# u added at a chunk's opening group from blocks on chip, w2's pieces at 2 KB, low parts a product later

## The chip, the cores and the metric

The kernel runs on one core of a Trainium2 chip. A core has a matrix engine (TensorE, PE in the rows; its weight loads are PEld), three element-wise engines (VectorE = DVE, ScalarE = ACT, GpSimd = POOL), a queue that issues DMAs (SyncE = SP) and 16 DMA engines that carry them between HBM and the on-chip memory. SBUF holds tiles of 128 partitions, PSUM the sums that TensorE makes. Each engine works through its own instructions in order and waits on semaphores for the others. The metric is the device time of one execution in microseconds (us).

## What is computed

Inputs are float64 arrays read as pairs of 32-bit words. An attention with random features gives `x` (8 x 576 rows of 512), and a mixing network follows:

```python
def phi(x):
    h = np.einsum('bhsd,md->bhsm', x, omega) - np.sum(x * x, axis=-1, keepdims=True) / 2.0
    return np.exp(h - np.max(h, axis=-1, keepdims=True)) / np.sqrt(m)
# attn = phi(q) (phi(k)^T v) / (phi(q) sum(phi(k)) + 1e-6), heads side by side: x
h = x.transpose(0, 2, 1) @ U @ V          # U: 576 x 32, V: 32 x 576
u = x + h.transpose(0, 2, 1)
out = u + np.maximum(u @ w_ch1, 0.0) @ w_ch2   # w_ch1: 512 x 2048, w_ch2: 2048 x 512
```

## The kernel before

The first 440 us are the attention; it leaves the rows of `u` in HBM (`u_dram`). The rest is the two-layer network over six chunks of 768 rows. A float32 factor stands as a high part (ACT casts it to fp32r) and a low part (the rest), and each product is three passes of TensorE: high x high, high x low, low x high. A pass of 384 columns is one MATMUL row of the trace.

Chunks 0 and 1 keep w2 on chip; chunk 1 writes the weights of both layers, already split and combined, to HBM: `wx_dram` (first layer) and `w2x_dram` (second, by `seconds`). Chunks 2 to 5, some 590 us, are the stage that the change is mostly about. There both layers are done by a scheme of seven block products in place of eight, and all weights are streamed: each chunk loads 56 tiles `wx` and 56 tiles `wy` of 256 KB, 8 buffers of each.

A chunk is 8 passes p over w1's columns. In pass p `products2` makes seven products i = 0 to 6 into two PSUM banks (`p_s`, called X and Y). I number them n = 7p + i within the chunk. Between them come sums that DVE takes out of PSUM (`near`: u2, u3, c22, c21, c12, in the order of products 1, 3, 4, 5, 6), and from these, after a relu, eight operands T of the second layer, each split into a high part (`halves`: ACT) and a low part (`low`: DVE for T1 and T3, POOL for the other five of seven). The bank of product 4 is needed by product 6, so product 6 waits for DVE's sum c22; product 5 waits for u3; the next pass's product 0 waits for c21 and its product 1 for c12.

Two passes make a group g = p // 2. Its second layer (`Group.block`) is woven into the two passes after it: behind product n of those two passes stands block s = n mod 14, six matmuls of the i-th second-layer product for half j of the columns; the order of i is 1, 3, 2, 5, 7, 6, 4, each for j = 0 and 1. A block's PSUM bank is taken out by `evict` into accumulators `acc[i, j]` (a1 to a7 below; they lie in `w1f` and `acc`): ACT copies in group 0, DVE adds in groups 1 and 2. Two of the i's are held in PSUM over all groups (4 and 6; rows `p_r`). Group 3's blocks stand in passes 0 and 1 of the next chunk; there the a's are combined by DVE and POOL to the four output blocks, and `Output` fetches u's rows again from HBM (16 DMAs of 96 KB in 128-byte pieces a chunk), transposes the sums (`yt`, L1349 and L1353), adds them to u (`uraw`) and stores the result (16 DMAs in 128-byte pieces).

SP's queue is in program order. At the end of slot n it has one `wy` load (for the group two passes ahead: load number k of a group is issued at least six slots before the block that reads it), one `wx` load (for product n + 7), and what `follow(n)` puts there: in chunks 3 to 5 fetches of u at n = 0, 1, 12 and 13, stores at n = 12, 13, 17 and 19. A store that waits for DVE holds every load behind it.

## Time and profile before

| | |
|---|---|
| median of 2 runs | 1161.53 us (1160.68 to 1162.38) |
| the profiled execution | 1159.5 us, its span 1157.7 us |
| PE busy | 1066.5 us (92%) |
| DVE, ACT, POOL busy | 803.0 (69%), 595.5 (51%), 611.3 (53%) us |
| DMA queue q1 | 490880 packets, 231.22 MB, 78.0% of 16 engines' span |
| mean granted TensorE clock | 0.978 |

PE is nearly full on the mean, so a stage is read by what its matmuls wait for. "Busy" of a matmul includes the end of its pipeline: matmuls of 384 columns start every 0.17 us in a row without waits while each is shown 0.33 us long. In chunk 2 to 5 the passes start at these times: chunk 2 at 570.6, chunk 3 at 694.4, chunk 4 at 838.2, chunk 5 at 982.4 us; the last group's blocks stand alone from 1118.3 us on (the tail). A releaser in the rows is what ended a wait.

### The profile page before, as it was taken

To read this page: it belongs to the slowest core of one execution; us is meant where nothing else is said; L and a number is where in the kernel's file an instruction comes from. 1 tells how busy PE (TensorE), PEld (TensorE's weight loads), DVE (VectorE), ACT (ScalarE), POOL (GpSimd) and SP (SyncE) were. 2 spreads that over 40 slices of the span, in tenths; PEclk is the share of its full clock that TensorE was granted. 3 is DMA by queue.
4 is the path that set the end of the run, shared out by engine and by line. 5 is a ranking of instruction groups with operands and counts; after the bars stand their busy time and mean duration, and the time that the engine had idled before them with its cause. 6 is when DMAs were issued, how large, how long until landed. Compare 5 with 4: busy or idle time off the path is not lost. (4 is left out here: it accounts for less than half of the span.)

```text
span 1157.7 us, 19949 instructions
## 1 busy us (share of the span) xinstructions
PE 1066.5 (92%) x6447; PEld 999.1 (86%) x6447; DVE 803.0 (69%) x1543; ACT 595.5 (51%) x1521; POOL 611.3 (53%) x582
## 2 busy tenths in 40 slices
PE   8999999999999999999879999799996899969993
PEld 7999999999889897898769988688886798869983
DVE  4898989989877757776743687535876358763554
ACT  5999898998656534333435343333433334333330
POOL 3447466583455564777435547444474444744552
PEclk9999999999999999999999999999999999999996
DMA  8899897893145654986688999699996999959876
GB/s 137 146 177 146 188 163 150 188 142 99 70 142 158 145 116 149 284 294 232 215 298 236 238 310 247 140 238 248 310 252 144 235 241 319 252 133 278 283 170 129
DMA packets 493350, 232.78 MB, mean 201 GB/s; under 512 B 379840, under 2 KB 439232, under 8 KB 493248
## 3 DMA queue, kind: packets, MB, share of 16 engines
q1 hardware_dynamic: 490880, 231.22, 78.0%
q8 instruction: 52, 0.85, 0.3%
q10 hardware_dynamic: 2368, 0.30, 0.2%
q14 instruction: 50, 0.41, 0.1%
HBM read 183.21 MB, written 48.23 MB: 200 GB/s over the span
## 5 line engine op out<-in xcount | busy, mean ns | idle before, releaser
L1094 PE MATMUL p_s<-ux,wx 128*128 128x384 f32 x1344 | 281.3, 345 | 35.1 <-DVE near L810 26.7
L1094 PEld LDWEIGHTS p_s<-ux,wx 128*128 128x128 f32 x1344 | 239.0, 192 | 52.6 <-DVE near L810 36.0
L1235 POOL TENSOR_TENSOR t<-near,t 128x384 fp32r<-128x384 f32 x128 | 137.5, 1094 | 238.1 <-ACT t L1054 238.1
L1279 PE MATMUL p_o<-t,wy 128*128 128x384 f32 x960 | 199.6, 343 | 24.4 <-DMA wy<-w2x_dram 21.6
L1279 PEld LDWEIGHTS p_o<-t,wy 128*128 128x128 f32 x960 | 173.2, 193 | 29.0 <-DMA wy<-w2x_dram 19.2
L589 ACT ACTIVATE e<-p_p,nm 128x128 f32<-128x128 f32 x576 | 167.6, 390 | 22.4 <-DVE nm L582 14.1
L810 DVE TENSOR_TENSOR near<-p_s,near 128x384 f32<-128x384 f32 x200 | 110.0, 551 | 80.7 <-PE p_s L1094 73.5
L436 POOL TENSOR_TENSOR xl<-xT,xh 128x384 fp32r<-128x384 f32 x95 | 94.2, 1012 | 111.7 <-ACT xh L432 94.3
L1058 ACT ACTIVATE near<-near 128x384 f32<-128x384 f32 x64 | 33.6, 525 | 212.1 <-DVE near L810 212.1
L582 DVE TENSOR_REDUCE nm<-p_p 128x4 f32<-128x512 f32 x144 | 97.7, 679 | 21.0 <-PE p_p L576 11.7
L574 PE MATMUL p_p<-omh,xh 128*128 128x256 f32 x288 | 92.4, 321 | 1.2 <-ACT e L589 0.9
L1054 ACT CAST t<-near 128x384 fp32r<-128x384 f32 x160 | 82.1, 515 | 21.4 <-POOL near L810 13.2
L1279 PE MATMUL p_r<-t,wy 128*128 128x384 f32 x384 | 79.5, 341 | 6.1 <-DMA wy<-w2x_dram 6.1
L575 PE MATMUL p_p<-oml,xh 128*128 128x256 f32 x288 | 81.3, 282 | 0.0
L576 PE MATMUL p_p<-omh,xl 128*128 128x256 f32 x288 | 81.0, 282 | 0.0
L810 DVE TENSOR_TENSOR w1f<-p_o,w1f 128x384 f32<-128x384 f32 x96 | 53.0, 552 | 37.1 <-PE p_o L1279 37.0
L1279 PEld LDWEIGHTS p_r<-t,wy 128*128 128x128 f32 x384 | 68.8, 192 | 7.9 <-DMA wy<-w2x_dram 7.9
L1028 PE MATMUL p_s<-ux,wx 128*128 128x384 f32 x336 | 70.2, 344 | 4.8 <-DVE near L810 3.0
L1028 PEld LDWEIGHTS p_s<-ux,wx 128*128 128x128 f32 x336 | 61.2, 190 | 11.9 <-DVE near L810 4.6
L976 PE MATMUL p_p<-ux,wx 128*128 128x384 f32 x384 | 71.2, 336 | 0.2 <-DVE g L985 0.2
L532 PE MATMUL p_n<-kv,eT 128*128 128x65 f32 x512 | 71.3, 269 | 0.1
L183 POOL TENSOR_TENSOR mag<-mag,low 128x512 int32<-128x512 int32 (+2 forms) x35 | 45.1, 1288 | 47.5 <-DVE mag L161 42.3
(166 smaller groups left out, 2309.2 us busy)
## 6 DMA issues: line engine op xcount, KB each, us to landing
wx<-wx_dram SPq DMA_DIRECT2D x224, 256.0 KB, 4.7
wy<-w2x_dram SPq DMA_DIRECT2D x224, 256.0 KB, 4.6
raw<-in_moe_w_ch_dram SPq DMA_DIRECT2D x32, 512.0 KB, 4.4
wx_dram<-wx SPq DMA_DIRECT2D x56, 256.0 KB, 2.1
uraw<-u_dram SPq DMA_DIRECT2D x136, 96.0 KB, 4.5
u_dram<-x SPq DMA_DIRECT2D x36, 256.0 KB, 2.2
qt<-in_q_dram SPq DMA_DIRECT2D x120, 72.0 KB, 3.2
kt<-in_k_dram SPq DMA_DIRECT2D x52, 144.0 KB, 4.9
```

The lines of the kernel that those rows point to most:

```text
L436: rest.tensor_tensor(out=self.xl[-1], in0=self.turned, in1=f32(self.xh[-1]), op=ALU.subtract)
L574: nc.tensor.matmul(o, part.xh[g][:, ts], oh, start=True, stop=False)
L575: nc.tensor.matmul(o, part.xh[g][:, ts], ol, start=False, stop=False)
L576: nc.tensor.matmul(o, part.xl[g][:, ts], oh, start=False, stop=True)
L582: nc.vector.tensor_reduce(out=self.nm[:, :n], in_=self.pp[:, :n], axis=AX.X, op=ALU.max, negate=True)
L589: nc.scalar.activation(out=self.e[:, j, :], in_=self.pp[:, j, :], func=AF.Exp, bias=self.nm[:, j : j + 1])
L810: keep(engine.tensor_tensor(out=out, in0=a, in1=b, op=op))
L1028: keep(nc.tensor.matmul(o, l, r, start=(i in (0, 1, 4, 5) and k + j == 0), stop=(k == 1 and j == 2), skip_group_check=True,))
L1054: keep(nc.scalar.copy(out=T[i][:, 0], in_=x))
L1094: keep(nc.tensor.matmul(o, l, r, start=(i in (0, 1, 4, 5) and k + j == 0), stop=(k == 1 and j == 2), skip_group_check=True,))
L1235: keep(nc.gpsimd.tensor_tensor(out=l, in0=x, in1=h, op=SUBTRACT))
L1279: keep(nc.tensor.matmul(bank, l, r, start=(n + m == 0 and not (held and self.g)), stop=(n == 1 and m == 2 and (not held or self.g == LAST) ...
```

## The change

1. **u from blocks on chip.** A chunk's own transposed blocks of u lie in `w1f` until its pass 4. Group 0's evictions now add them: for i = 3, 2, 4, 5 DVE adds (or subtracts) the bank and a block, where ACT copied; for i = 7 ACT copies. Held in PSUM are now 1 and 6 instead of 4 and 6; 1's banks are copied by ACT at group 3 (`f1`), and POOL's sums of group 3 are rewritten (12 a chunk instead of 10). `Output` becomes `output`: transposes straight into the tile that is stored, no fetch, no add, at n = 11, 12, 15 and 17. In chunk 1 all six tiles of u are fetched before the stores, where two waited for stores of others.
2. **w2's pieces.** `w2x_dram` is laid out so that a `wy` load reads 2 KB a partition in one piece instead of twice 1 KB; chunk 1's writes go in 1 KB pieces instead of 2 KB.
3. **Low parts one product later.** DVE's low parts (of T1 and T3, and in passes 0 and 1 of chunks 3 to 5 T2's, which POOL had) are issued behind the next product's eviction, or at product 6 behind c12.
4. DVE's sums in SBUF take the form scalar_tensor_tensor (`exact`), and in chunk 1 four of seven operand splits go to POOL.

```diff
@@ split, sums
     def split(hl, x, rest=nc.gpsimd):
         keep(nc.scalar.copy(out=hl[:, 0], in_=x))
-        keep(rest.tensor_tensor(out=hl[:, 1], in0=x, in1=f32(hl[:, 0]), op=SUBTRACT))
+        if rest is nc.vector:
+            exact(hl[:, 1], x, f32(hl[:, 0]), SUBTRACT)
+        else:
+            keep(rest.tensor_tensor(out=hl[:, 1], in0=x, in1=f32(hl[:, 0]), op=SUBTRACT))
...
-    w2x_dram = [dram.tile([P, 2, 7, 2 * P], F32, name=f"w2x_dram{p}") for p in range(NH)]
+    w2x_dram = [dram.tile([P, 7, 2, 2 * P], F32, name=f"w2x_dram{p}") for p in range(NH)]
...
-            sums(self.s[i], a, b, op)
+            exact(self.s[i], a, b, op)
...
-            sums(self.total(i if self.c == 1 or i < 4 else 2), a, b, SUBTRACT, nc.gpsimd if self.c == 1 and i < 4 else nc.vector)
+            to = self.total(i if self.c == 1 or i < 4 else 2)
+            if self.c == 1 and i < 4:
+                sums(to, a, b, SUBTRACT, nc.gpsimd)
+            else:
+                exact(to, a, b, SUBTRACT)
...
-            split(slots[i], x, nc.vector)
+            split(slots[i], x, nc.gpsimd if self.c == 1 and i in (1, 3, 4, 6) else nc.vector)
@@ products2
-                low(rest, T[i][:, 1], x, f32(T[i][:, 0]))
+                step = lambda: low(rest, T[i][:, 1], x, f32(T[i][:, 0]))
+                if rest < 3:
+                    lows.append(step)
+                else:
+                    step()
...
-                    halves(2, c21, 3)
+                    halves(2, c21, third)
                 elif i == 6:
                     sums(c12, X, u2, ADD)
+                    while lows:
+                        lows.pop(0)()
...
-                evict = slot(i)
+                evict, due = slot(i), lows[:]
                 after(i)
                 if i in (0, 1) and pend:
                     pend.pop(0)()
                 evict()
+                for step in due if i < 6 else ():
+                    lows.pop(0)()
@@ Group
-                    keep(nc.sync.dma_start(out=f32(w), in_=w2x_dram[2 * self.g + n][:, :, PLACE[i], :]))
+                    keep(nc.sync.dma_start(out=f32(w), in_=w2x_dram[2 * self.g + n][:, PLACE[i]]))
...
-            held = i in (4, 6)
+            held = i in (1, 6)
...
         def evict(self, i, j, bank):
+            chunk = self.chunk
             if self.g < LAST:
+                if i in (1, 6):
+                    return
+                if self.g:
+                    sums(acc[i, j], bank, acc[i, j], ADD)
+                elif i == 7:
+                    keep(nc.scalar.copy(out=acc[i, j], in_=bank))
+                else:
+                    x = chunk.total(3) if i == 3 else chunk.block(*{2: (0, 0), 4: (1, 0), 5: (1, 1)}[i])
+                    sums(acc[i, j], bank, parted(x[:, j]), SUBTRACT if i == 3 else ADD)
                 return
+            a = {n: acc[n, j] for n in (2, 3, 4, 5, 7)}
+            pool = lambda x, y: sums(x, x, y, ADD, nc.gpsimd)
             if i == 1:
+                chunk.f1[j] = parted(dec.tile([P, HT], F32, name="f1", tag="mag", bufs=2))
+                keep(nc.scalar.copy(out=chunk.f1[j], in_=bank))
+                pool(a[2], chunk.f1[j])
+                pool(a[5], chunk.f1[j])
+            elif i == 6:
+                for n in (3, 5, 4):
+                    sums(a[n], bank, a[n], ADD)
             else:
+                sums(a[i], bank, a[i], ADD)
+                if i == 5:
+                    pool(a[3], a[5])
+                elif i == 7:
+                    pool(a[5], a[7])
+                    pool(a[7], chunk.f1[j])
+                    pool(a[4], a[7])
@@ follow, and the end
             def follow(n):
-                if n in (0, 1):
-                    out.fetch(n)
-                if n in (8, 9, 12, 13, 16, 17, 18, 19):
-                    out.add(*before.outs.pop(0), nc.vector)
-                if n in (12, 13):
-                    out.fetch(n - 10)
+                if n in (11, 12, 15, 17):
+                    output(c - 1, (11, 12, 15, 17).index(n))
...
+            group.T.append(now.products2(pairs, slot, between, low, pend, 2 if c > 2 and p < 2 else 3))
...
-    for m in range(4):
-        out.fetch(m, m > 1)
     for s in range(14):
         done.block(s)()
         next(loads, None)
+        if s in (11, 12):
+            output(NCH - 1, s - 11)
+    for m in (2, 3):
+        output(NCH - 1, m, True)
```

Three places of the order matter below. The first is SP's queue in passes 1 and 2 of chunk 3 (the others are alike): `out_dram` are stores of the chunk before, `uraw<-u_dram` the fetches of u, the `wx` and `wy` loads those for pass 2 on. Before:

```order
L1261 DMA wy<-w2x_dram_5403 128x2x256
L866 DMA wx<-wx_dram_5_5429 128x512
L1340 DMA out_dram<-uraw 32x24x32 x4
L376 DMA uraw<-u_dram_68 32x24x32 x4
L1261 DMA wy<-w2x_dram_5402 128x2x256
L866 DMA wx<-wx_dram_6_5430 128x512
L1340 DMA out_dram<-uraw 32x24x32 x4
L376 DMA uraw<-u_dram_68 32x24x32 x4
L1261 DMA wy<-w2x_dram_5403 128x2x256
L866 DMA wx<-wx_dram_0_5431 128x512
```

and in the change:

```order
L1355 DMA out_dram<-uraw 32x24x32 x4
L1279 DMA wy<-w2x_dram_5403 128x512
L869 DMA wx<-wx_dram_5_5429 128x512
L1355 DMA out_dram<-uraw 32x24x32 x4
L1279 DMA wy<-w2x_dram_5402 128x512
L869 DMA wx<-wx_dram_6_5430 128x512
L1279 DMA wy<-w2x_dram_5403 128x512
L869 DMA wx<-wx_dram_0_5431 128x512
```

The fetches between the loads are gone, and the first store stands one slot earlier, ahead of the loads of slot 12.

The second is DVE in pass 1 of chunk 3, from u3 (the first `near`) over c22 (the second) to c21 (the third). Before:

```order
L810 TENSOR_TENSOR near<-p_s,near 128x384
L810 TENSOR_TENSOR w1f<-p_r,w1f 128x384 x2
L810 TENSOR_TENSOR w1f<-p_r,w1f 128x2x192
L810 TENSOR_TENSOR near<-p_s,near 128x384
L1233 SCALAR_TENSOR_TENSOR t_9716<-near,t_9716 128x384
L810 TENSOR_TENSOR w1f<-p_r,w1f 128x384 x2
L810 TENSOR_TENSOR w1f<-p_r,w1f 128x2x192
L810 TENSOR_TENSOR near<-p_s,near 128x384
```

and in the change:

```order
L816 TENSOR_TENSOR near<-p_s,near 128x384
L816 TENSOR_TENSOR w1f<-p_r,w1f 128x384 x2
L816 TENSOR_TENSOR w1f<-p_r,w1f 128x2x192
L1251 SCALAR_TENSOR_TENSOR t_9656<-b_9593,t_9656 128x384
L816 TENSOR_TENSOR near<-p_s,near 128x384
L816 TENSOR_TENSOR w1f<-p_r,w1f 128x384 x2
L816 TENSOR_TENSOR w1f<-p_r,w1f 128x2x192
L1347 STREAM_TRANSPOSE uraw<-acc 128x384
L1347 STREAM_TRANSPOSE uraw<-w1f 128x384
L816 TENSOR_TENSOR near<-p_s,near 128x384
```

T1's low part (`t<-b`), which stood ahead of u3 two sums earlier, now stands between the sums of i = 6 (`p_r`, the third is a7 before and a4 now) and c22; T3's (`t<-near`) has gone behind c21, and two transposes of the output stand ahead of c21.

The third is POOL in the same pass, from the last low part of pass 0's operands on (`t`); `w1f` are its sums of group 3. Before:

```order
L1235 TENSOR_TENSOR t_11021<-near,t_11021 128x384
L810 TENSOR_TENSOR w1f<-w1f 128x384 x2
L1235 TENSOR_TENSOR t_11051<-near,t_11051 128x384
L810 TENSOR_TENSOR w1f<-w1f 128x384 x2
L1235 TENSOR_TENSOR t_11075<-near,t_11075 128x384
L810 TENSOR_TENSOR w1f<-w1f 128x384
L810 TENSOR_TENSOR w1f<-w1f 128x2x192
L810 TENSOR_TENSOR w1f<-w1f 128x384
L810 TENSOR_TENSOR w1f<-w1f 128x2x192
```

and in the change:

```order
L1253 TENSOR_TENSOR t_10985<-near,t_10985 128x384
L816 TENSOR_TENSOR w1f<-w1f 128x384
L1253 TENSOR_TENSOR t_11014<-near,t_11014 128x384
L816 TENSOR_TENSOR w1f<-w1f 128x384
L1253 TENSOR_TENSOR t_11037<-near,t_11037 128x384
L816 TENSOR_TENSOR w1f<-w1f 128x384
L816 TENSOR_TENSOR w1f<-w1f,f_10844 128x2x192
L816 TENSOR_TENSOR w1f<-w1f 128x2x192
L816 TENSOR_TENSOR w1f<-w1f 128x384
L816 TENSOR_TENSOR w1f<-w1f,f_10868 128x2x192
L816 TENSOR_TENSOR w1f<-w1f 128x2x192
```

DVE's third addition of half 0 (to a7 before, to a4 now) waits for POOL: counted from the `t` that opens the first of fourteen POOL operations in a row (t2, five slots earlier), its sum was the twelfth and is now the eleventh.

## Rows read from the trace of the kernel before

**Rows 1.** Table by stretch; columns in its first row; share is of DMA.

```profile
core 0: us, PE busy (x) PEld busy (x) DVE busy (x) ACT busy (x) POOL busy (x), PEclk, DMA share, GB/s
440.00:570.60 130.60, 125.00 (x607) 110.39 (x605) 98.50 (x158) 49.40 (x112) 86.38 (x81) 0.99 0.71 242
...
838.20:874.50 36.30, 30.82 (x168) 28.89 (x168) 26.07 (x42) 12.28 (x24) 26.06 (x24) 1.00 0.86 225
874.50:982.40 107.90, 94.68 (x504) 89.48 (x504) 62.59 (x107) 40.34 (x82) 47.67 (x42) 0.97 0.90 241
...
1018.80:1118.30 99.50, 91.20 (x504) 89.47 (x505) 51.97 (x92) 37.81 (x78) 45.75 (x43) 0.97 0.80 230
1074.70:1089.20 14.50, 14.50 (x85) 14.50 (x84) 8.05 (x14) 5.50 (x11) 7.63 (x8) 1.00 0.92 287
```

**Rows 2.** Waits of PE from 874.5 to 982.4: us in total, times, longest.

```profile
PE p_o L1279 <- DMA wy<-w2x_dram: 6.5, 3, 4.4
PE p_s L1094 <- DMA wx<-wx_dram: 2.8, 3, 2.1
```

**Rows 3.** SP's queue, chunk 4: start, us, line, transfer (xcount).

```profile
876.04 2.13 SPq L1340 DMA_DIRECT2D out_dram<-uraw  x4
880.83 2.02 SPq L376 DMA_DIRECT2D uraw<-u_dram  x4
...
891.67 0.54 SPq L1261 DMA_DIRECT2D wy<-w2x_dram  x1
```

**Rows 4.** PE in order of time, chunk 4; in brackets the idle time before.

```profile
870.91 1.32 PE L1094 MATMUL p_s<-ux,wx 128*128 128x384 f32 x6 [2.10 <-DVE near L810]
...
874.53 1.31 PE L1094 MATMUL p_s<-ux,wx 128*128 128x384 f32 x6 [1.24 <-DVE near L810]
...
894.99 1.33 PE L1279 MATMUL p_o<-t,wy 128*128 128x384 f32 x3 [4.42 <-DMA wy<-w2x_dram]
896.12 2.07 PE L1094 MATMUL p_s<-ux,wx 128*128 128x384 f32 x6
```

**Rows 5.** DVE in order of time, chunk 4, passes 0 and 1.

```profile
861.02 1.37 DVE L810 TENSOR_TENSOR uraw<-yt,uraw 128x384 f32<-128x384 f32 x1
862.31 1.36 DVE L1233 SCALAR_TENSOR_TENSOR t<-b,t 128x384 fp32r<-128x384 f32 x1
...
869.84 0.56 DVE L810 TENSOR_TENSOR w1f<-p_r,w1f 128x384 f32<-128x384 f32 x1 [0.52 <-POOL w1f L810]
870.31 0.55 DVE L810 TENSOR_TENSOR near<-p_s,near 128x384 f32<-128x384 f32 x1
...
872.53 1.48 DVE L810 TENSOR_TENSOR w1f<-p_r,w1f 128x384 f32<-128x384 f32 x3
...
874.85 0.57 DVE L1349 STREAM_TRANSPOSE yt<-w1f 128x384 f32<-128x384 f32 x1
```

**Rows 6.** POOL in order of time, the end of the chain of fourteen.

```profile
867.73 4.12 POOL L810 TENSOR_TENSOR w1f<-w1f 128x384 f32<-128x384 f32 x4
```

**Rows 7.** DMA queue 1131 to 1136, `wy` loads alone: packets, MB, share.

```profile
q1 hardware_dynamic: 1531, 1.36, 97.5%
```

**Rows 8.** DMA queue 589.5 to 592, nearly all 2 KB pieces.

```profile
q1 hardware_dynamic: 512, 0.93, 101.7%
```

**Rows 9.** DMA queue 1146 to 1156, stores in 128-byte pieces.

```profile
q1 hardware_dynamic: 11121, 1.40, 92.0%
```

**Rows 10.** DVE in chunk 2, pass 0.

```profile
588.99 0.69 DVE L1142 TENSOR_TENSOR u<-p_kv,u 128x512 f32<-128x512 f32 x1 [3.35 <-DMA u<-u_dram]
```

**Rows 11.** PE in chunk 1.

```profile
449.78 1.40 PE L1028 MATMUL p_s<-ux,wx 128*128 128x384 f32 x6 [1.77 <-DVE g L985]
```

**Rows 12.** Waits of PE in the tail, from 1118 on.

```profile
PE p_o L1279 <- DMA wy<-w2x_dram: 5.3, 1, 5.3
```

**Rows 13.** POOL in the tail.

```profile
1135.32 8.26 POOL L810 TENSOR_TENSOR w1f<-w1f 128x384 f32<-128x384 f32 x8 [8.25 <-DVE w1f L810]
```

**Rows 14.** SP in the tail.

```profile
1144.03 4.95 SPq L1340 DMA_DIRECT2D out_dram<-uraw  x8
```

## What the change should do to the time, and why

> **What bounds the kernel now.** I read the table by stretch first, to see where PE loses time, then what ended its waits there, and then the queues of the engines that it waited for. All comparisons go by a stretch's own clean pass: in chunk 5 a pass of 84 matmuls runs without a wait in 14.50 us [rows 1]. A chunk of eight would take 116 us; chunks 3, 4 and 5 take 143.8, 144.2 and 135.9 us by the pass starts above. So PE's waits in these three cost some 76 us, and that is the target, not PE's mean of 92%.
>
> In chunk 4 the two halves lose differently [rows 1]. Passes 0 and 1 take 36.3 us for 29.0 clean, over by 7.3, at a clock of 1.00. Passes 2 to 7 take 107.9 for 87.0, over by 20.9, and chunk 5's take 99.5, over by 12.5. Chunk 3 differs from chunk 4 by 0.4 us in all, so I treat it as the same. In passes 2 to 7 most of the listed waits are for loads: 6.5 us for `wy`, 2.8 for `wx` [rows 2]. The loads are late because of SP. It stands until 876.04 for the first store of the old chunk's output, whose data DVE must first add to u, then until 880.83 for a buffer whose stores must land before u can be fetched again, and by 891.67 has issued the `wy` load that PE wanted at about 890 [rows 3]. PE stands 4.42 us there, and its next six matmuls take 2.07 us instead of 1.32 or less [rows 4]: after a long gap the clock is lower for a while, and the 0.97 of the stretch [rows 1] says the same.
>
> In passes 0 and 1 the releaser is DVE: product 6 of pass 1 waits 2.10 us for c22, pass 2's first product 1.24 for c21 [rows 4]. Behind DVE stands POOL: the chain of fourteen ends at 871.85, four operations in 4.12 us [rows 6], so the twelfth ends about 869.8, and DVE's sum a7 begins at 869.84, just ahead of c22 at 870.31 [rows 5].
>
> **The loads, chunks 3 to 5.** Removed are 16 fetches of 96 KB and 8 additions on DVE of 0.56 to 1.37 us a chunk [rows 5]. First the queue. In the change the first store needs two transposes, 0.57 us each [rows 5], behind the sums of i = 6, half 1. c22 ends about 871.0 (below), two sums bring 871.95, the third waits for POOL's last at 871.85 and ends near 872.4, the transposes near 873.6. So SP stands until 873.6 instead of 876.04, and no fetch waits for a landing behind it: two stores of four DMAs (2.13 us each [rows 3]) and three pairs of loads, some 1.2 us each (0.54 for the `wy` load [rows 3], about as much for the `wx` load), bring the load that was issued at 891.67 forward to about 881, nine microseconds ahead of its use.
>
> Then the DMA engines, which must also carry it. A `wy` load in 1 KB pieces takes 0.94 us of all 16 (5.0 us x 97.5% for 1.36 MB, 256 KB a load [rows 7]). In 2 KB pieces the nearest rows are 2.5 us x 101.7% for 0.93 MB, 0.72 us a load [rows 8]. 96 KB in 128-byte pieces take 0.65 us (10 us x 92.0% for 1.40 MB [rows 9]). From slot 11 to slot 27 there are 17 pairs, 24.5 us, 16 stores, 10.4, and eight fetches for the next chunk, 5.2: 40.1 us, about 42 at 95% use. PE takes 17 x 12 matmuls x 0.173 = 35.3 us. The loads fall 6.8 us behind, of which their lead (six slots and more, held back by the stand of SP) covers some 4; lateness is 0 to 6.8, and I take 2.5. With 16 fetches more and 1 KB pieces it would be 10.4 + 17 x 0.22 = 14 us worse, about what the trace of before loses.
>
> A page of the Trainium skill speaks against part of this. "DMA: Bandwidth & Descriptors", section "Specifications", puts the least transfer for full rate at 512 B, by which 1 KB and 2 KB pieces are alike. By the rows they differ, 0.94 to 0.72 us; by the rule the 3.7 us of these 17 loads would stay, three times, and the time would be 11 us longer.
>
> In passes 2 to 7 I therefore leave 5 us of the 20.9 (2.5 of lateness, 1.2 for c21, 1.0 for c12 and little else), 5 in chunk 3 too, and 3.5 of chunk 5's 12.5, which has no next chunk to fetch for. The gain is 15.5 + 15.9 + 9.0 = **40.4 us**.
>
> **Passes 0 and 1, chunks 3 to 5.** I cost this at a small loss. Product 6 needs c22. Its chain is one POOL operation of 1.03 us shorter, so a4 can begin about 868.8 and end at 869.35. But T1's low part now stands between: 1.36 us with POOL running beside it [rows 5], 0.56 at the shortest form seen there; I take 1.1. c22 at 0.55 [rows 5] ends at 871.0; before, product 6 began at 870.91 [rows 4]. The matmuls ahead of it wait a little less, so the gap grows from 2.1 to some 2.5, and may pull the clock down (2.07 for 1.32 per six matmuls [rows 4]). c21 loses T3's low part ahead of it and gets two transposes: three sums of 0.5 each ended at 874.0 before [rows 5], now the two transposes end at 873.6 and c21 at 874.1, as before within 0.4. c12 has a low part and the transposes of the second output tile ahead: 874.1 + 0.56 + 0.5 + 1.14 + 0.55 = 876.9 or later, against a next product that would start near 876; that is the 1.0 above. Low parts behind evictions cost PE nothing otherwise while ACT and POOL, which T's other parts use, are 34% busy on ACT and 72% on POOL there [rows 1]. Without that cover each would cost its 0.56 to 1.36. I allow 1 us a chunk for the clock: **-3 us**, bounds 0 and -8.
>
> **DVE's evictions.** In group 0 eight copies go from ACT to DVE, minus two (i = 1, now held): at 0.55 us [rows 5] some 4.4 us a chunk, in passes where DVE is 58% busy [rows 1] and gives up additions of 4.5 to 11 us. Hidden; uncovered it is rival 3.
>
> **Chunk 2.** DVE waits 3.35 us there for u tiles fetched late [rows 10], and PE behind it, with a lower clock after. All six tiles now precede the stores. I take 3.35 + 0.9 for the clock, and 0.25 for low parts: **4.5 us** (bounds 2 and 7).
>
> **Chunk 1.** PE waits 1.77 us for a sum g behind DVE's operand splits [rows 11]; four of seven go to POOL (86.38 busy of 130.6 us [rows 1]). **2 us** (0 and 4). The writes of `w2x_dram` in 1 KB pieces cost DMA engines time: 56 pieces of 256 KB at 0.22 more, 12 us, where they are 71% busy [rows 1]; costed at nothing, hidden by the idle 38 us, and up to 12 if they meet a load that PE waits for.
>
> **The tail.** PE's 5.3 us wait for `wy` [rows 12] goes with the 16 fetches in front of it. The end doesn't move as far, since POOL's sums come last: eight in 8.26 us from 1135.32 on [rows 13], and the first store is issued at 1144.03 [rows 14]. Four of twelve sums now need only i = 1's bank and fall before. The stores themselves take 12.6 us from their start to the end at 1157.7 (16 at 0.65 is 10.4), and stay. I take **3.5 us** (2 and 7).
>
> **The sum.** 40.4 - 3 + 4.5 + 2 + 3.5 = 47.4 us from the profiled 1159.5 gives 1112.1. The median of the runs shown is 2.0 above that execution; I keep 1112 for the median of after.
>
> **The rivals.**
>
> 1. *Passes 0 and 1 get faster too.* If a low part takes 0.56 and the shorter POOL chain comes through, half of the 7.3 goes in three chunks and the 3 us loss doesn't come: 1112 - 14 = 1098; all of it, 1112 - 3 - 22 = 1087. For it: DVE is rid of additions of 1.37 us there [rows 5]. Against: product 6 still hangs on the eleventh of fourteen POOL operations.
> 2. *The loads stay late.* SP still stands for DVE, now one slot earlier, and the DMA engines have 42 us of work for 35. If half of the 40.4 stays: 1132. This holds also the case that the fetches gone free nothing because the stores alone hold the queue.
> 3. *DVE becomes the bound.* If the 4.4 us of evictions, and the two T2 low parts a chunk moved from POOL (2 x 1.36), come out in PE's waits in four chunks, 4 x 7 = 28: 1140.
> 4. *The form of DVE's sums costs.* Some eleven sums a chunk of 0.56 to 1.36 us [rows 5] take a form with a scalar; if each took twice as long and stood on the path in chunks 1 to 4, 4 x 11 x 0.95 (the middle) = 42: 1154. Against: a sum of two SBUF operands took 1.37 as plain addition and 1.36 in the scalar form, side by side [rows 5]. The Trainium skill has the rule, "Vector Engine (DVE) Microarchitecture Reference", "Points that are easy to get wrong": the scalar form with two SBUF sources that are not bf16 runs at half throughput. The trace does not agree for this shape.
> 5. *Slower: the two output buffers.* Output tile m2 takes the buffer of m0, and its transposes on DVE wait until m0's stores have landed, with every eviction and c-sum queued behind, so PE stops. Before, landing came 4.8 us after issue (876.04 to 880.83 [rows 3]); then it held SP alone. Now m0 lands near 873.6 + 4.8 = 878.4, and DVE reaches m2 at slot 15, near 880.6, 2.2 us later. Each microsecond of landing beyond 7 stops PE. To be slower than 1161.5 it must take 50 us, or 16 a chunk in three chunks: landing at 23 us. At DMA engines already 90% busy [rows 1] a few are possible, 16 hardly.
>
> **Chances.** Forecast 0.62 (its own range 1100 to 1122), rival 1 0.15, rival 2 0.13, rival 3 0.05, rival 4 0.02, rival 5 0.03. The range of 8 in 10 is 1088 (all of rival 1's waits gone) to 1138 (rival 2 with the uncertain clock). About 2% is what a measurement of this kernel can tell from no change: faster means under 1138.3, slower over 1184.8. Faster: the forecast, rival 1, most of rival 2 and some of 3, 0.88. The same: the rest of 2 and 3, rival 4 and half of 5, 0.10. Slower: 0.02.
>
> **What the profile after would show.** Right: passes 2 to 7 of chunk 4 near 92 us instead of 107.9, with PE's waits for `wy` and `wx` there under 3 us; the `wy` load that came 15.6 us after a chunk's first store (876.04 to 891.67) now some 8 us after it; `wy` loads of 2 KB packets; in chunk 2's pass 0 no wait of DVE for `u`; in pass 1 product 6 still waiting over 2 us for c22, and pass 2's product 1 some 1 us for c12; the tail's first store some 3 us earlier, counted from the tail's start. Wrong: passes 0 and 1 under 34 us (rival 1), `wy` waits over 6 us a chunk (rival 2), waits for evictions in passes 2 and 3 (rival 3), transposes of the output that DVE holds for a landing store (rival 5).

## The result, and the profile after

The changed kernel takes **1110.43 us** (median of 2 runs, 1109.66 to 1111.19) against 1161.53: ratio 0.956, 95% interval 0.9519 to 0.9601, 51.1 us faster. The profiled execution has a span of 1109.4 us, 48.3 below the 1157.7 of before. The forecast was 1112, in a range of 1088 to 1138. One execution of run 12 below, its profiled one, ran at a granted clock of 0.66 throughout and took 1441 us; it is left out of that run's median.

The page of the changed kernel, its head (busy us, share of the span, instructions) and the row of the main DMA queue:

```profile
PE 1051.0 (95%) x6447; PEld 992.9 (89%) x6447; DVE 782.7 (71%) x1537; ACT 585.9 (53%) x1497; POOL 620.1 (56%) x588
...
q1 hardware_dynamic: 418176, 224.92, 76.9%
```

PE does the same 6447 matmuls in 95% of the span where it was 92%. The queue carries 6.3 MB less (231.22 to 224.92), and 72,700 packets fewer: without 64 fetches of u in 128-byte pieces, and with `wy` loads in pieces twice as long.

Where the time went is best told by stage. This table is worked out from the starts of the first matmuls of the passes in both traces; "forecast" are the terms of the sum.

| stage | before | after | moved | forecast |
|---|---|---|---|---|
| up to chunk 2 | 570.6 | 572.1 | +1.5 | -2 |
| chunk 2 | 123.8 | 115.4 | -8.4 | -4.5 |
| chunks 3, 4, 5, passes 0 and 1 | 36.5, 36.3, 36.4 | 35.9, 35.9, 35.1 | -2.3 | +3 |
| chunks 3, 4, 5, passes 2 to 7 | 107.3, 107.9, 99.6 | 93.7, 95.2, 90.3 | -35.6 | -40.4 |
| tail | 39.4 | 35.8 | -3.6 | -3.5 |
| all | 1157.7 | 1109.4 | -48.3 | -47.4 |

The sum came out within a microsecond, but by errors that cancel: passes 2 to 7 and the stage up to chunk 2 gave 8.3 us less than forecast, chunk 2 and passes 0 and 1 gave 9.2 more. The experiments are mostly about these four. The trace is of one execution: runs 5, 6 and 7 below leave the work of chunks 3 to 5 as it is (run 5 but for the form of DVE's sums), and there passes 2 to 7 take 277.6, 277.8 and 276.2 us in all, where the table has 279.2 (93.7 + 95.2 + 90.3). So that row gave 35.6 to 38.6 us, short of its 40.4 each time, and a difference of 3 us in it is scatter.

The table by stretch of the changed kernel answers to [rows 1]: chunk 4's passes 0 and 1, its passes 2 to 7, and the tail.

```profile
core 0: us, PE busy (x) PEld busy (x) DVE busy (x) ACT busy (x) POOL busy (x), PEclk, DMA share, GB/s
...
817.10:853.00 35.90, 31.55 (x169) 30.55 (x169) 23.31 (x41) 13.14 (x27) 26.94 (x25) 0.95 0.59 192
853.00:948.20 95.20, 91.25 (x505) 88.56 (x505) 59.83 (x108) 37.46 (x74) 45.95 (x41) 0.98 0.98 271
...
1073.60:1109.40 35.80, 15.30 (x85) 14.33 (x84) 13.69 (x29) 2.81 (x6) 18.09 (x19) 0.80 0.48 103
```

In passes 2 to 7 the DMA engines are now 98% busy, and in passes 0 and 1 only 59% (86% in [rows 1]): the fetches of u are gone from there. What PE still waits for in chunk 4's passes 2 to 7 (us in total, times, longest), against 6.5 us for `wy` and 2.8 for `wx` in [rows 2], and 2.1 more for `wy` in a line of the same view of before that [rows 2] leave out. That line first, then those of the change:

```profile
PE p_r L1279 <- DMA wy<-w2x_dram: 2.1, 2, 1.7
```

```profile
PE p_s L1110 <- DMA wx<-wx_dram: 2.9, 4, 2.0
PE p_s L1110 <- DVE near L816: 1.1, 1, 1.1
PE p_r L1297 <- DMA wy<-w2x_dram: 0.8, 1, 0.8
```

3.7 us of loads are left, of 11.4. Behind the longest, at the end of pass 4, six matmuls take 1.93 us as in [rows 4]; the granted clock of pass 4 is 0.91.

```profile
900.47 1.93 PE L1110 MATMUL p_s<-ux,wx 128*128 128x384 f32 x6 [1.97 <-DMA wx<-wx_dram]
```

SP's queue in chunk 4 (start, us, transfer), the place of [rows 3]: the loads behind slot 11, the first store, the second, and the two `wy` loads that were issued at 882.89 and 891.67 before.

```profile
845.84 0.43 SPq L869 DMA_DIRECT2D wx<-wx_dram  x1
852.49 2.14 SPq L1355 DMA_DIRECT2D out_dram<-uraw  x4
854.73 0.50 SPq L1279 DMA_DIRECT2D wy<-w2x_dram  x1
855.27 0.66 SPq L869 DMA_DIRECT2D wx<-wx_dram  x1
856.03 3.29 SPq L1355 DMA_DIRECT2D out_dram<-uraw  x4
859.42 0.47 SPq L1279 DMA_DIRECT2D wy<-w2x_dram  x1
```

The first store comes 35.4 us into the chunk (852.49 - 817.1), where the working had 873.6 - 838.2 = 35.4. The second `wy` load comes 6.9 us after it, where it came 15.6 us after in [rows 3]. But SP still stands from 846.27 to 852.49, 6.1 us of it for DVE's transposes, with loads behind it.

PE and DVE in pass 1 of chunk 4, the places of [rows 4] and [rows 5]:

```profile
849.50 1.32 PE L1110 MATMUL p_s<-ux,wx 128*128 128x384 f32 x6 [1.44 <-DVE near L816]
852.96 1.33 PE L1110 MATMUL p_s<-ux,wx 128*128 128x384 f32 x6 [1.08 <-DVE near L816]
```

```profile
847.64 0.56 DVE L816 TENSOR_TENSOR w1f<-p_r,w1f 128x384 f32<-128x384 f32 x1 [1.62 <-POOL w1f L816]
848.11 0.86 DVE L1251 SCALAR_TENSOR_TENSOR t<-b,t 128x384 fp32r<-128x384 f32 x1
848.90 0.55 DVE L816 TENSOR_TENSOR near<-p_s,near 128x384 f32<-128x384 f32 x1
```

The order is the one described: a4, T1's low part, c22. The gap of product 6 is 1.44 us (2.10 before), that for c21 1.08 (1.24).

The two passes moved in opposite ways. In chunk 4 pass 0 takes 18.4 us where it took 17.4, and pass 1 17.6 where it took 19.0. Product 1 of pass 0 waits for c12, first before, then in the change:

```profile
841.66 1.32 PE L1094 MATMUL p_s<-ux,wx 128*128 128x384 f32 x6 [1.12 <-DVE near L810]
```

```profile
821.23 1.39 PE L1110 MATMUL p_s<-ux,wx 128*128 128x384 f32 x6 [1.82 <-DVE near L816]
```

### The profile page after: what moved, and what is told of

Its sections match the earlier page's. It is cut to its first block, busy times and chain, and to the rows that moved or that the text cites. A ratio compares the mean times of both kernels' runs of the same rounds, so it can differ in the third digit from the quotient of the medians.

```text
span 1109.4 us, 19835 instructions
## 1 busy us (share of the span) xinstructions
PE 1051.0 (95%) x6447; PEld 992.9 (89%) x6447; DVE 782.7 (71%) x1537; ACT 585.9 (53%) x1497; POOL 620.1 (56%) x588
## 3 DMA queue, kind: packets, MB, share of 16 engines
q1 hardware_dynamic: 418176, 224.92, 76.9%
## 4 chain that ended last, share of the span: by engine, by line
PE 30%; POOL 7%; DVE 5%; DMA 4%; issue 2%; ACT 1%; SPq 1%; POOLq 0%; DVEq 0%; ACTq 0%
PE p_s L1110 15%; PE p_o L1297 11%; PE p_r L1297 3%; POOL w1f L816 3%; DMA wx<-wx_dram 2%; POOL t L1253 2%; DVE near L816 1%; POOL near L816 1%; DMA wy<-w2x_dram 1%; DVE ux L806 1%; DVE uraw L1347 1%; DVE t L1251 1%; DVE w1f L816 0%; ACT ux L809 0%; DVE b L1247 0%
## 5 line engine op out<-in xcount | busy, mean ns | idle before, releaser
L1110 PE MATMUL p_s<-ux,wx 128*128 128x384 f32 x1344 | 274.5, 339 | 24.0 <-DVE near L816 14.6
L1110 PEld LDWEIGHTS p_s<-ux,wx 128*128 128x128 f32 x1344 | 236.0, 189 | 35.9 <-DVE near L816 21.3
L1253 POOL TENSOR_TENSOR t<-near,t 128x384 fp32r<-128x384 f32 x122 | 130.8, 1092 | 171.8 <-ACT t L1064 171.8
L1297 PE MATMUL p_o<-t,wy 128*128 128x384 f32 x960 | 193.0, 336 | 2.9 <-DVE acc L816 2.7
L1297 PEld LDWEIGHTS p_o<-t,wy 128*128 128x128 f32 x960 | 169.4, 189 | 4.2 <-DVE acc L816 3.3
L436 POOL TENSOR_TENSOR xl<-xT,xh 128x384 fp32r<-128x384 f32 x95 | 94.2, 1011 | 113.2 <-ACT xh L432 89.8
L816 DVE TENSOR_TENSOR w1f<-p_o,w1f 128x384 f32<-128x384 f32 x120 | 66.4, 553 | 61.0 <-PE p_o L1297 60.9
L1037 PE MATMUL p_s<-ux,wx 128*128 128x384 f32 x336 | 70.3, 344 | 5.0 <-DVE near L816 2.6
L1037 PEld LDWEIGHTS p_s<-ux,wx 128*128 128x128 f32 x336 | 61.1, 190 | 12.7 <-DVE near L816 4.6
L816 POOL TENSOR_TENSOR near<-near,b 128x384 f32<-128x384 f32 x32 | 42.5, 1328 | 52.3 <-DVE b L1247 52.3
```

The source lines that it names most:

```text
L436: rest.tensor_tensor(out=self.xl[-1], in0=self.turned, in1=f32(self.xh[-1]), op=ALU.subtract)
L816: keep(engine.tensor_tensor(out=out, in0=a, in1=b, op=op))
L1037: keep(nc.tensor.matmul(o, l, r, start=(i in (0, 1, 4, 5) and k + j == 0), stop=(k == 1 and j == 2), skip_group_check=True,))
L1110: keep(nc.tensor.matmul(o, l, r, start=(i in (0, 1, 4, 5) and k + j == 0), stop=(k == 1 and j == 2), skip_group_check=True,))
L1253: keep(nc.gpsimd.tensor_tensor(out=l, in0=x, in1=h, op=SUBTRACT))
L1297: keep(nc.tensor.matmul(bank, l, r, start=(n + m == 0 and not (held and self.g)), stop=(n == 1 and m == 2 and (not held or self.g == LAST) ...
```

## The experiments

Each run's time is a median, with the kernel before run beside it on the same chip; that was 1160.5, 1161.1, 1159.6 and 1161.1 us in the four groups of runs. Two theories were held against each other. **Loads**: most of the gain is that the streamed weights of chunks 3 to 5 come in time. **DVE**: it is DVE's order (additions gone, low parts later) that gives PE its operands sooner. Within the first, a second question: are loads late because the DMA engines have too much to carry, or because SP issues them too late?

The stages of seven runs that take one thing away or do one alone, us (from the pass starts, as above):

| stage | before | 2 KB alone | part 1 alone | after | 1 KB | low parts at once | c1 on DVE | u late | fetches back |
|---|---|---|---|---|---|---|---|---|---|
| up to chunk 2 | 570.6 | 572.1 | 572.0 | 572.1 | 571.8 | 571.3 | 570.6 | 571.6 | 572.6 |
| chunk 2, passes 0, 1 | 33.3 | 33.3 | 33.4 | 27.7 | 27.6 | 30.6 | 27.6 | 32.3 | 27.8 |
| chunk 2, passes 2 to 7 | 90.5 | 88.5 | 90.7 | 87.7 | 89.5 | 88.6 | 87.7 | 87.7 | 87.7 |
| chunk 4, passes 0, 1 | 36.3 | 36.4 | 37.4 | 35.9 | 35.1 | 37.4 | 35.9 | 36.0 | 35.9 |
| chunks 3 to 5, passes 2 to 7 | 314.8 | 303.2 | 286.4 | 279.2 | 288.3 | 280.0 | 277.8 | 276.2 | 284.4 |
| tail | 39.4 | 39.3 | 36.2 | 35.8 | 36.4 | 35.6 | 36.0 | 36.5 | 37.0 |

**1. The 2 KB pieces alone** (the kernel before with part 2):

```diff
-    w2x_dram = [dram.tile([P, 2, 7, 2 * P], F32, name=f"w2x_dram{p}") for p in range(NH)]
+    w2x_dram = [dram.tile([P, 7, 2, 2 * P], F32, name=f"w2x_dram{p}") for p in range(NH)]
...
-                    keep(nc.sync.dma_start(out=f32(w), in_=w2x_dram[2 * self.g + n][:, :, PLACE[i], :]))
+                    keep(nc.sync.dma_start(out=f32(w), in_=w2x_dram[2 * self.g + n][:, PLACE[i]]))
```

> The kernel before with part 2 alone: w2's streamed pieces at 2 KB (and the writes in chunk 1 at 1 KB); everything else as before. Theory A (the loads of chunks 3 to 5 are late because the DMA engines have more work than time, and 1 KB pieces cost 0.94 us a load where 2 KB pieces cost 0.72): lateness in passes 2 to 7 falls by 3 to 4 us a chunk, 1161.5 - 11 = 1150 us (1145 to 1156). Theory B (SP, standing for DVE and for landings, issues the loads too late, the engines are not the limit): 1159 to 1162 us, no change. By the Trainium skill's rule (DMA: Bandwidth & Descriptors, Specifications, full rate from 512 B on) also no change.

Measured 1148.69 us, ratio 0.9903 (0.9874 to 0.9931), 11.8 us less: one per cent, but clear of no change, and run 3 shows it the other way round. The 11.6 us of chunks 3 to 5's passes 2 to 7 are nearly all of it, 3.9 us a chunk on the mean, where 17 loads at 0.22 come to 3.7. What the DMA engines carry does count, and pieces of 1 KB and 2 KB are not alike.

**2. Part 1's core alone** (the changed kernel with everything else undone: 1 KB pieces, low parts at once, plain sums, chunk 1's splits on DVE, u's tiles in the old order):

```diff
-            held = i in (4, 6)
+            held = i in (1, 6)
...
-                if n in (0, 1):
-                    out.fetch(n)
-                if n in (8, 9, 12, 13, 16, 17, 18, 19):
-                    out.add(*before.outs.pop(0), nc.vector)
-                if n in (12, 13):
-                    out.fetch(n - 10)
+                if n in (11, 12, 15, 17):
+                    output(c - 1, (11, 12, 15, 17).index(n))
```

> The kernel before with part 1's core alone: u added from blocks at the opening group, no fetch of u for the output, POOL's rewritten sums; w2 in 1 KB pieces, low parts not deferred, plain sums, chunk 1's splits on DVE and u's tiles in the old order. Theory A: SP's stands and 16 x 0.65 us of fetches go, so most of the 35.5 us gained in passes 2 to 7 of chunks 3 to 5 and the tail's 3.6 are there: 1161.5 - 28 = 1133 us (1125 to 1140), and the 2 KB pieces bring the rest. Rival: the pieces and the low parts carry it, and this part alone gives less than 15 us: over 1146 us.

Measured 1133.69 us, ratio 0.9775 (0.9748 to 0.9802), 26.8 us less. 28.4 us of it are in passes 2 to 7 and 3.2 in the tail. In passes 0 and 1 it loses 1.0 us a chunk. That is the size that I had allowed, but by luck: my loss was to come from T1's low part between a4 and c22, and this run issues low parts at once.

**3. The changed kernel with 1 KB pieces** (the reverse of run 1):

> The changed kernel with w2's pieces back at 1 KB. Theory A: 0.22 us more for each of 17 loads in the crowded stretch, three chunks, so about 11 us: 1121 us (1116 to 1127), with PE's waits for wy and wx up by 2 to 4 us a chunk in passes 3 to 6. Theory B (without the stands the loads have slack, or pieces of 512 B and more are alike): 1110 us within 2.

Measured 1120.54 us, ratio 0.9655 (0.9634 to 0.9675), 10 us more than the change. 9.1 us of it stand in passes 2 to 7 of chunks 3 to 5, 1.8 in chunk 2, where my sum had no term for the pieces. The writes of `w2x_dram` in chunk 1 are back at 2 KB here, and the stage up to chunk 2 is the same within 0.3 us: costing those writes at nothing was right as far as that stage's scatter (2 us, run 6) lets one see.

**4. Low parts at once** (part 3 undone):

```diff
-                if rest < 3:
+                if rest < 0:
                     lows.append(step)
...
-            group.T.append(now.products2(pairs, slot, between, low, pend, 2 if c > 2 and p < 2 else 3))
+            group.T.append(now.products2(pairs, slot, between, low, pend, 3))
```

> The changed kernel with part 3 undone: low parts of T1 and T3 issued at once, T2's on POOL in passes 0 and 1. My prediction costed part 3 as a small loss at pass 1 (T1's low part now stands between a4 and c22): then undoing it gives 1107 to 1111 us, and product 6 of pass 1 waits under 1.2 us. Rival: an undeferred low part waits on DVE for ACT's cast and holds the eviction behind it, which PE feels in passes 0 and 1 of chunk 2 and in the passes 2 to 4: 1115 to 1122 us.

Measured 1120.64 us, ratio 0.9656 (0.9636 to 0.9676), 10 us more than the change: my expectation fell, the rival stands. The run undoes two things at once, the deferring and, in passes 0 and 1 of chunks 3 to 5, the move of T2's low part from POOL to DVE. 3.8 us are in chunk 2, where T2's low part did not move, so these are the deferring alone; 1.5, 1.5 and 2.3 are in passes 0 and 1 of chunks 3 to 5. PE and DVE of this kernel at the end of pass 1 of chunk 4:

```profile
853.88 1.32 PE L1110 MATMUL p_s<-ux,wx 128*128 128x384 f32 x6 [1.77 <-DVE near L816]
859.15 2.29 PE L1110 MATMUL p_s<-ux,wx 128*128 128x384 f32 x6 [2.91 <-DVE near L816]
```

```profile
853.28 0.55 DVE L816 TENSOR_TENSOR near<-p_s,near 128x384 f32<-128x384 f32 x1
855.03 1.29 DVE L1251 SCALAR_TENSOR_TENSOR t<-near,t 128x384 fp32r<-128x384 f32 x1 [1.20 <-ACT t L1064]
856.24 1.47 DVE L816 TENSOR_TENSOR w1f<-p_r,w1f 128x384 f32<-128x384 f32 x3
857.64 0.56 DVE L1347 STREAM_TRANSPOSE uraw<-acc 128x384 f32<-128x384 f32 x1
858.13 0.53 DVE L1347 STREAM_TRANSPOSE uraw<-w1f 128x384 f32<-128x384 f32 x1
858.59 0.51 DVE L816 TENSOR_TENSOR near<-p_s,near 128x384 f32<-128x384 f32 x1
```

T3's low part stands idle 1.20 us for ACT's cast, then takes 1.29 us, and the three sums, two transposes and c21 are behind it: pass 2's first product waits 2.91 us, and its six matmuls take 2.29 us. In the change that low part has gone behind c21, and the wait is 1.08 us. So part 3 takes out of c21's way the low part's duration and, as much again, a wait for another engine at the head of DVE's queue. The trace of the kernel before shows the same wait, between c22 and the three sums of [rows 5]; the working did not price it:

```profile
872.05 0.56 DVE L1233 SCALAR_TENSOR_TENSOR t<-near,t 128x384 fp32r<-128x384 f32 x1 [1.20 <-ACT t L1054]
```

**5. The plain form of DVE's sums:**

```diff
-            exact(hl[:, 1], x, f32(hl[:, 0]), SUBTRACT)
+            keep(rest.tensor_tensor(out=hl[:, 1], in0=x, in1=f32(hl[:, 0]), op=SUBTRACT))
...
-            exact(self.s[i], a, b, op)
+            sums(self.s[i], a, b, op)
...
-                exact(to, a, b, SUBTRACT)
+                sums(to, a, b, SUBTRACT)
```

> The changed kernel with the plain two-operand form again for DVE's sums of two SBUF operands that the change had moved to the scalar form (weights' sums, prepare, operand splits). My prediction: the forms cost the same, 1110 us within 2. In chunk 1 of the changed kernel two such sums of 768 columns took 1.89 and 2.06 us beside POOL where they took 0.94 and 0.96 before. Theory 'neighbour' (any form is slow while POOL works on the same kind of operands): they stay near 1.9 here. Theory 'form' (the scalar form alone gives way to POOL): 0.95 here, and 3 to 6 us in all are gained: 1105 to 1107 us.

Measured 1110.32 us, ratio 0.9558 (0.9539 to 0.9578), the change's own time. The form makes no difference. In chunk 1, beside POOL's splits, the plain form is as slow as the other (of the two sums that the expectation names, the one of 1.89 us has 768 columns, the one of 2.06 us 256); first this kernel's row, then those of the change:

```profile
447.00 1.89 DVE L816 TENSOR_TENSOR uraw<-ux,ux 128x768 f32<-128x768 f32 x1
```

```profile
446.13 1.89 DVE L806 SCALAR_TENSOR_TENSOR uraw<-ux,ux 128x768 f32<-128x768 f32 x1
449.61 0.56 DVE L994 SCALAR_TENSOR_TENSOR g<-p_s,g 128x384 fp32r<-128x384 f32 x1 [1.59 <-ACT g L993]
```

**6. Chunk 1's splits on DVE again:**

```diff
-            split(slots[i], x, nc.gpsimd if self.c == 1 and i in (1, 3, 4, 6) else nc.vector)
+            split(slots[i], x, nc.vector)
```

> The changed kernel with chunk 1's seven operand splits all on DVE again. My prediction gave the move to POOL 2 us, so undoing it would give 1112 us and a wait of 1.8 us before the first sum g as before. Rival, from the trace of the change (the wait for g is 2.28 us there, longer than the 1.77 of before, with DVE's sums at 1.9 us beside POOL): the move gains nothing, 1109 to 1110 us.

Measured 1106.88 us, ratio 0.9529 (0.951 to 0.9548), 3.5 us less than the change's median; the intervals of the two ratios overlap. The same sum takes half as long without POOL beside it:

```profile
446.55 0.94 DVE L806 SCALAR_TENSOR_TENSOR uraw<-ux,ux 128x768 f32<-128x768 f32 x1
```

PE's wait for the first sum g is 1.8 us as in [rows 11], where the change has 2.3; this run first, then the change:

```profile
449.88 2.13 PE L1037 MATMUL p_s<-ux,wx 128*128 128x384 f32 x6 [1.76 <-DVE g L994]
```

```profile
450.22 2.25 PE L1037 MATMUL p_s<-ux,wx 128*128 128x384 f32 x6 [2.28 <-DVE g L994]
```

The move to POOL therefore gains nothing in chunk 1. How much it costs I can't say closer than 0 to 3.5 us: the stage up to chunk 2 takes 570.9 to 572.9 us in the seven traces with the splits on POOL and 570.6 to 572.3 in the six with them on DVE, and part of the difference stands in later chunks that the edit does not touch.

**7. u's tiles late** (chunk 1's fetches in the old order):

```diff
                     todo = [lambda t=t, po=po: self.store(t, po)]
+                    if self.c and t < 2:
+                        todo.append(lambda t=t: self.residual(t + 4))
...
-                for t in range(CT):
+                for t in range(4):
```

> The changed kernel with chunk 1's tiles of u fetched in the old order (the last two behind stores of others). By my term for chunk 2: 3.35 us of DVE's wait and a clock drop come back in chunk 2's pass 0, 1114 to 1115 us, passes 0 and 1 of chunk 2 at 31 to 32 us instead of 27.7. Rival: with low parts deferred the waiting DVE holds less that PE needs, and under 1.5 us comes back: 1110 to 1112 us.

Measured 1113.18 us, ratio 0.958 (0.9565 to 0.9596). Chunk 2's passes 0 and 1 take 32.3 us instead of 27.7: 4.6 us, where the term was 3.35 + 0.9. The total rises by 2.7 only; in the traced execution passes 2 to 7 of chunks 3 to 5 were quicker by 3.0, which is their scatter.

**8. The fetches back as transfers alone:**

```diff
...
+                if n in (0, 4, 8, 13):
+                    m = (0, 4, 8, 13).index(n)
+                    fetch(c - 1, {m: late["dum"].tile([P, TOK], F32, name="dum", bufs=1)})
```

> The changed kernel with the 16 fetches of u a chunk put back as transfers alone, at slots 0, 4, 8 and 13, into a tile that nothing reads: no addition on DVE, no buffer whose stores must land, no store that waits longer. It tells the fetches' own price on the DMA engines (10.4 us a chunk) and in SP's queue (four times 2 us) from that of the stands. Theory 'engines': the loads fall behind as without 2 KB pieces, 3 us a chunk and more: 1119 to 1125 us. Theory 'stands' (DVE's additions and landings ahead of the loads made them late; passes 0 and 1 have room on the engines, busy 59% there): 1110 to 1114 us.

Measured 1118.57 us, ratio 0.9636 (0.9619 to 0.9653), 8 us more than the change, between the two theories and nearest to the engines'. It brings back 48 fetches, those of chunks 3 to 5; the 16 of the tail stay away. 5.2 us are in passes 2 to 7, 1.2 in the tail. PE's waits for loads from chunk 3 on, all of them:

```profile
PE p_o L1298 <- DMA wy<-w2x_dram: 6.1, 5, 2.2
PE p_r L1298 <- DMA wy<-w2x_dram: 3.6, 3, 1.8
PE p_s L1110 <- DMA wx<-wx_dram: 3.5, 6, 1.3
```

13.2 us, where the change has 8.1 (2.7 for `wy`, 5.4 for `wx`). So the fetches' transfers, with SP's issue of them, are worth some 8 us in a kernel whose `wy` loads come in 2 KB pieces, of the 27 us that part 1 gave at 1 KB. By difference the rest went with what stood around them, DVE's additions and the landings ahead of the loads; no run takes these two away alone, and at 1 KB the transfers may have cost more.

**9. An improved order**, three edits: chunk 1's splits on DVE; the sum for operand 5 two products earlier and each split's DVE half one product later; in the tail DVE adds i = 1's bank itself, the first output goes ahead of two of the three sums of i = 6, and half of the stores go out from ACT's queue.

```diff
-            if self.made == 5:
+            if self.made == (5 if self.c == 1 else 3):
                 self.prepare(4)
...
-            split(slots[i], x, nc.gpsimd if self.c == 1 and i in (1, 3, 4, 6) else nc.vector)
+            if self.c > 2:
+                self.flush()
+                hl = slots[i]
+                keep(nc.scalar.copy(out=hl[:, 0], in_=x))
+                self.rest.append(lambda: exact(hl[:, 1], x, f32(hl[:, 0]), SUBTRACT))
+            else:
+                split(slots[i], x, nc.vector)
...
+                if end:
+                    sums(a[2], bank, a[2], ADD)
+                    sums(a[5], bank, a[5], ADD)
...
-            keep(nc.sync.dma_start(
+            keep((nc.scalar if queue and a % 2 else nc.sync).dma_start(
```

> An improved version of the changed kernel, three edits in three places that the table by stage tells apart. (a) Chunk 1's splits all on DVE, as the run that did this alone: 2 to 3 us. (b) In the last pass of chunks 2 to 4 the sum for operand 5 is made two products earlier and each DVE split stands one product later, so that DVE doesn't wait for ACT's cast ahead of c12: the 2.0 us of product 1 and the clock behind it go, passes 0 and 1 of chunks 3 to 5 at 33 to 34 us instead of 35.1 to 35.9. (c) In the tail DVE adds i = 1's bank itself where POOL added a copy, the first output tile needs one sum of i = 6 only, and half of the stores are issued from ACT's queue: PE's 3.0 us go and the tail takes 28 to 31 us instead of 35.8. In all 1110.4 - 2.5 - 6 - 6 = 1096 us (1091 to 1101). Rival: the waits move on (ACT's cast to the next split, the tail to POOL's chain), half of it: 1102 to 1106 us.

Measured 1090.7 us, ratio 0.9402 (0.9387 to 0.9418), 20 us less than the change. Passes 0 and 1 of chunks 3 to 5 take 32.4, 32.3 and 32.3 us, the tail 29.9. All of the gain in passes 0 and 1 is in pass 0, 14.6 us in each of the three chunks. The rows show again a wait at the head of DVE's queue. In the change, at the start of chunk 4, DVE waits 0.95 us for ACT's cast ahead of c12 (the second `near`), and PE's product 1 waits 1.82 us for c12 (821.23 above):

```profile
816.45 0.55 DVE L816 TENSOR_TENSOR near<-p_s,near 128x384 f32<-128x384 f32 x1
816.91 0.55 DVE L816 TENSOR_TENSOR w1f<-p_o,w1f 128x384 f32<-128x384 f32 x1
817.38 0.55 DVE L1251 SCALAR_TENSOR_TENSOR t<-near,t 128x384 fp32r<-128x384 f32 x1
817.84 0.95 DVE L806 SCALAR_TENSOR_TENSOR w1f<-w1f 128x768 f32<-128x768 f32 x1
819.75 0.96 DVE L806 SCALAR_TENSOR_TENSOR ux<-w1f,ux 128x768 fp32r<-128x768 f32 x1 [0.95 <-ACT ux L809]
820.62 0.55 DVE L816 TENSOR_TENSOR near<-p_s,near 128x384 f32<-128x384 f32 x1
```

An eviction and a deferred low part stand there between c21 and the operand's sum (817.84), which before came right behind c21 (837.58 and 838.04). In the improved order DVE runs there without a wait, and the granted clock of passes 0 and 1 of chunk 4 is 1.00 (0.95 in the change):

```profile
809.70 0.95 DVE L806 SCALAR_TENSOR_TENSOR ux<-w1f,ux 128x768 fp32r<-128x768 f32 x1
810.57 0.55 DVE L816 TENSOR_TENSOR near<-p_s,near 128x384 f32<-128x384 f32 x1
```

```profile
810.40:842.70 32.30, 29.58 (x169) 28.95 (x169) 21.72 (x39) 11.86 (x25) 27.19 (x25) 1.00 0.67 215
```

**10. Stores behind their transposes** (the changed kernel; transposes at slots 11, 12, 16, 18, their stores at 13, 14, 17, 19):

```diff
...
-                if n in (11, 12, 15, 17):
-                    output(c - 1, (11, 12, 15, 17).index(n))
+                if n in (13, 14, 17, 19):
+                    ready.pop(0)()
+                if n in (11, 12, 16, 18):
+                    ready.append(output(c - 1, (11, 12, 16, 18).index(n)))
```

> The changed kernel with the stores of the output issued one to two slots behind their transposes in SP's queue (transposes at slots 11, 12, 16 and 18, stores at 13, 14, 17 and 19), so that SP doesn't stand for DVE with loads behind it. If SP's stands (18.2 us listed in three chunks) still make the loads late: PE's waits for loads in passes 2 to 4 go, 3 to 5 us less: 1105 to 1107 us. If the DMA engines are the limit there (100% busy in passes 3 to 6): 1110 us within 2, and the waits come later in the same passes.

Measured 1102.32 us, ratio 0.9512 (0.9491 to 0.9532), 8 us less than the change. Passes 2 to 7 take 89.8, 90.0 and 88.1 us, 87.0 being clean. In the four traces of kernels that leave this work as it is they take 276.2 to 279.2 in all, here 267.9. The waits of PE there in chunk 4, and the stretch's row, which names a busy share of DMA of 1.00:

```profile
PE p_s L1110 <- DVE near L816: 1.1, 1, 1.1
PE p_s L1110 <- DMA wx<-wx_dram: 0.6, 2, 0.4
```

```profile
847.10:937.10 90.00, 89.08 (x505) 87.16 (x505) 60.16 (x108) 37.60 (x74) 45.81 (x41) 1.00 1.00 280
```

In chunk 4 the first store goes out 0.5 us before pass 2 begins, in the change (852.49, the pass at 853.0) as here (846.64, 847.1). But two more pairs of loads have gone ahead of it, and two more ahead of each of the other three. SP's stands for DVE's transposes fall from 18.2 us in the three chunks to 0.7, and the DMA share of passes 0 and 1 of chunk 4 rises from 0.59 to 0.68. That took away 3.1 of the 3.7 us that PE waited for loads. The engines are 100% busy and carry the same loads, and these are in time: what still made them late was SP's stand. (The last two transposes move by a slot as well; PE's wait for DVE in passes 2 to 7 of chunk 4 stays at 1.1 us.)

**11. Both.** Runs 9 and 10 in one kernel:

> The improved order together with the stores issued behind their transposes. If the two gains are of different waits (DVE's order in passes 7 to 1 and the tail; SP's stands in passes 2 to 5), they add: 1090.7 - 8 to 11 = 1080 to 1083 us, passes 2 to 7 of chunks 3 and 4 at 88 to 90 us. Rival: with less waiting in passes 0 and 1 the DMA engines become the bound and the loads are late again: 1086 to 1090 us.

Measured **1086.48 us**, ratio 0.9358 (0.9341 to 0.9375), the fastest of all, 24 us below the change. But the gains do not add, 4.2 us beside run 9 where 8 came alone, and the time is in the rival's range. Passes 2 to 7 take 90.6, 90.7 and 88.2 us (92.4, 93.1 and 89.5 in run 9). There was less to gain: from chunk 3 on PE waits 6.8 us for loads in run 9 and 2.4 in run 11, against 8.1 in the change and 0.6 in run 10. That the DMA engines are the bound for the 2.4, as the rival says, is not shown.

**12. DVE adds i = 1's bank in chunks 3 to 5 too** (the edit against run 11):

```diff
-                if end:
+                if True:
                     sums(a[2], bank, a[2], ADD)
```

> The same, and in chunks 3 to 5 too DVE adds i = 1's bank to a2 and a5 itself where POOL added ACT's copy: four POOL operations of a chunk's chain of fourteen go, four on DVE of 0.55 us come at slots 0 and 1. Theory: PE's waits for c22 and c21 in pass 1 (1.6 and 1.3 us) hang on POOL's chain, so 2 to 3 us a chunk go: 6 to 8 us less than the run beside it, pass 0 and 1 at 30 us. Rival: DVE has no room at slots 0 and 1 and c12 and u2 come later there: within 2 us of the run beside it, or slower.

Measured 1087.57 us, ratio 0.9368 (0.9345 to 0.9392): no gain over run 11. Its trace can't be laid beside that of run 11, so whether the waits for c22 and c21 went and something else came, or they stayed, is open.

## Why the prediction was right, and where it was not

**The bound and the mechanism** were read rightly: chunks 3 to 5 lost their time to loads held back, and most of the gain is there. Runs 1 and 3 give the pieces 11.8 and 10 us where the working had 11, and run 2 gives part 1 28.4 us in passes 2 to 7 where the rest of the 40.4 is 29. Run 8 finds some 8 us for the fetches' transfers alone.

**Passes 2 to 7: 35.6 us instead of 40.4.** The queue's working held to the decimal for the first store, in part by luck: in chunk 4 pass 1 began 1.0 us later than forecast (18.4 us into the chunk for 17.4), and a4 came 1.0 us sooner in it. What failed is the step "their lead (six slots and more, held back by the stand of SP) covers some 4; lateness is 0 to 6.8, and I take 2.5". I put the lateness that stays down to the DMA engines' work, and took SP's stand for a detail of it. Run 10 takes the stand away and leaves the work: 8 to 11 us come in these stretches (267.9 us against 276.2 to 279.2). Loads stood behind a store at the end of pass 1, while the engines were 59% busy, and later ones were late up to pass 4. The mark "passes 2 to 7 of chunk 4 near 92" was missed by 3.2 us; "`wy` and `wx` under 3 us" by 0.7. The rest of the 3.2 has no term in the sum, which left "little else": pass 4 alone, at a granted clock of 0.91, takes 19.0 us, 4.5 over a clean pass, and PE waits 2.2 of these. And the 1.2 for c21 was put into the wrong stage, since that wait ends as pass 2 starts.

**Passes 0 and 1: 2.3 us gained instead of 3 lost.** The working of the sums was close for c21 (1.08 us waited, 1.24 before). For product 6 it had T1's low part at 1.1 us (0.86) and a4's start 13.2 us into the pass (868.8 - 855.6); a4 started at 12.2 (847.64 - 835.4), mostly because POOL's operations of this chain took 1.0 us each up to there. Before, some took 1.2 to 1.3 while DVE made the additions that are gone and T1's low part (861.02 and 862.31 in [rows 5]); POOL's rows of the kernel before, and one of the change:

```profile
860.96 2.30 POOL L810 TENSOR_TENSOR w1f<-w1f 128x384 f32<-128x384 f32 x2
863.22 1.33 POOL L1235 TENSOR_TENSOR t<-near,t 128x384 fp32r<-128x384 f32 x1
```

```profile
840.52 1.01 POOL L816 TENSOR_TENSOR w1f<-w1f 128x384 f32<-128x384 f32 x1
```

The wait came to 1.44 instead of some 2.5 us, and the six matmuls behind it take 1.32 us, not 2.07. The 1.0 us for c12 in pass 2 didn't come: product 1 doesn't wait there. A longer wait for c12 came in pass 0, for which the working had no term: product 1 waits 1.82 us (1.12 before), and the pass is 1.0 us longer in chunks 3 and 4. Run 9 takes that wait away.

**Part 3 was mis-sized.** "Low parts behind evictions cost PE nothing otherwise" is where it stands: I priced only what a deferred low part delays, and not the 1.20 us for which T3's stood idle ahead of c21. Run 4 shows 10 us the other way, 3.8 of them in chunk 2, where my term had 0.25. With run 3's 1.8 us of pieces this more than covers what chunk 2 gave over its 4.5: taken away one at a time, u's tiles, low parts and pieces cost 4.6 + 3.8 + 1.8 = 10.2 us there, where the change gave 8.4, so they overlap. The term for u's tiles itself was right (4.6 in run 7, 4.25 forecast), though the mark "no wait of DVE for `u`" was not met: one of 2.06 us stands in pass 0 of chunk 2, which PE does not feel.

**Chunk 1: no gain instead of 2 us.** The step failed that moves DVE's work to POOL and counts DVE's time as freed: DVE's next sum took 1.89 us beside POOL for 0.94, ACT's casts stand behind that sum and DVE's part of g behind ACT (449.61 in run 5), so g came later, not sooner. The stage's +1.5 itself is within its scatter (run 6), and the 400th matmul already starts 1.6 us later, before any line that the change touches.

**The tail: 3.6, forecast 3.5.** PE's 5.3 us [rows 12] went and the matmuls end 6.9 us sooner after the tail's start, but the first store only 4.3 us (21.4 us after it instead of 25.7), and DVE's two waits for POOL's sums of i = 1's copy cost PE 2.7 us. The stores, which were to stay at 12.6 us, take 14.4 from the first issue to the end; counted in the same way they took 13.7 before (1157.7 - 1144.03).

**The rivals.** Rival 1 came in small part, 0.8 us a chunk where it had 3.6. Rival 2 is there in a mild form, and run 10 puts it down to SP's stand for DVE. Rivals 3 and 4 are excluded: from chunk 2 on PE waits for no eviction before the tail, and run 5 shows the forms equal; the rule of the Trainium skill named there ("Vector Engine (DVE) Microarchitecture Reference", "Points that are easy to get wrong") doesn't hold for these shapes. Rival 5 didn't come: no transpose waits for a landing.

## What to carry to other kernels

Look at what stands at the head of an in-order queue and for whom it waits: a low part that waits 1.2 us for a cast, or a store that waits for a transpose, delays all that is queued behind it. Moving low parts one product back (and T2's to DVE) gained 10 us here, moving stores two slots back 8. A DMA share of 100% isn't a bound by itself; ask whether the loads were issued as early as their buffers allowed. What the engines carry counts all the same (runs 1, 3 and 8). When work goes from DVE to POOL, price DVE's neighbours at their duration beside POOL.

## What the runs showed of the hardware

A sum of two SBUF operands of 128x768 takes 0.94 us on DVE and 1.89 us while POOL works on its own two, whichever form it has (the change, runs 5 and 6); of 128x384 0.56 and up to 1.37 [rows 5]. The Trainium skill ("SBUF — State Buffer", "SBUF: two separate sides") gives a cause: DVE with two SBUF inputs and a POOL operation that reads SBUF take turns at a shared pair of ports. The rows agree that they hold each other up, for both forms; that it is by taking turns at ports, no row here shows.

A 256 KB load in pieces of 2 KB a partition instead of 1 KB was worth 10 to 12 us over the 224 loads of `wy` (runs 1 and 3). By the Trainium skill's 512 B ("DMA: Bandwidth & Descriptors", "Specifications") it would have been worth nothing; here the runs decide.
